# State recurrence in pairs of steps, first loads on two queues and a new engine order, in a kernel that joins windowed attention with a diagonal state-space model

## The chip, the core and the metric

The kernel runs on one core of a Trainium2 chip. The core has five engines that run their own instruction streams and wait for each other by semaphores: TensorE (PE: matmuls, with its weight loads shown apart as PEld), VectorE (DVE), ScalarE (ACT), GpSimd (POOL) and SyncE (SP, which here only issues transfers). Sixteen DMA engines move data. The metric is the time of one execution in microseconds (us), the median over runs.

## The reference

Two independent branches, their outputs joined along the last axis, in bfloat16. S = L = 2048 tokens, D = 448, 16 heads of 28.

```
# A: attention over 8 positions, two apart
q, k, v = split(x @ wqkv)
logits[s, w] = q[s] . k[s - 2w] * 28**-0.5        (w = 0..7, masked where s - 2w < 0)
a = softmax(logits) @ v[s - 2w] @ wo
# B: a complex diagonal recurrence of 448 states
Lam_bar = exp(exp(log_dt) * (Lambda_re + 1j*Lambda_im))
B_bar = ((Lam_bar - 1) / Lam)[:, None] * Bmat
h[t] = Lam_bar * h[t-1] + B_bar @ x[t]
y[t] = 2 * real(Cmat @ h[t]) + x[t] * Dskip
```

## The kernel before

**Branch A.** A's tokens are brought into the layout features x tokens (`xT`, the first 1024 by transposes on TensorE: `XI`, `XA`, `XH`; the rest by transposing DMAs). `QK` and `QS` project to q and k, `qk` and `qh` evict them from PSUM to SBUF, and `P` multiplies, on VectorE, q with k shifted by 2w, for four shifts at once: 28 products of 128x2048. `E_` sums these over each head on TensorE, `lt`, `TR`, `tr` transpose the logits, `sma`, `smb`, `smc` are the softmax, `AL`, `al`, `ad`, `sp` turn the weights into a banded matrix by way of DRAM, `AV` multiplies it with v (`V_`), and `W_` applies wo; `w` evicts and `ow` stores.

**Branch B.** The 448 complex states are 7 groups `g` of 64; real and imaginary parts stand in 128 partitions. The 2048 steps are 512 columns of T = 4 steps, `j` = 0..3. `BU` projects x with B for one step (four steps in two passes of two PSUM banks), and `BR` adds the state of the step before, rotated by Lam_bar (a 128x128 matrix `R[g, 0]`), so that each bank holds the state as if the column began at zero. `z` evicts it. The last step of each pair of columns is joined (`UP`, with the rotation by four steps) and scanned along the 256 pairs by VectorE: `sa` turns into a rotating frame, `sb` is the scan with real decay, `sd` turns back; one call serves two groups (0 and 1, 2 and 3, 4 and 5, and 6 alone). Then the carried state is given back: `DN` and `dn` to the odd columns, and for each of the steps j = 0, 1, 2 a matmul `H_` (128x512) with its own rotation and a VectorE addition `h` (128x512 out of PSUM): 21 of each. `C` multiplies the states of one step and 128 columns with C (7 matmuls of 448 columns, summed in one bank), `c` adds x * Dskip (`xd`) on VectorE and `oc` stores. `ca`, `cs` scale C by Lam's coefficients; `pb` to `pg` compute all coefficients from the three vectors Lambda_re, Lambda_im and log_dt (`raw`); `ty`, `tf`, `ts` make the tables of the rotating frame, `rb` the rotations.

**Order.** Nothing is scheduled by a tool: the string `ORDER` lists every step once, with the PSUM banks it takes behind `@`, and a last `.` (ScalarE) or `=` (VectorE) says who evicts. Each engine runs its own steps in this order, without overtaking. SyncE issues nearly all transfers, in order too: x of the first four token blocks in two transfers, wqkv in slices of 128 columns, and so on; the three parameter vectors are issued by ScalarE as its first work. `WU` is 24 matmuls on zeros at the start.

Of the kernel before, what the change touches and what calls it, by code (L numbers as in the profile page):

```python
# [9 lines left out]
BF16 = mybir.dt.bfloat16  # L10
# [16 lines left out]
SHR = 1.0 - 1e-6  # L27
MAGIC = 12582912.0
# [4 lines left out]
BD WU@0 XI0@12 XI1 xa00= xa01. PP@3 pcopy pa pb pd_ xh0. QS00@4 XH1@5 pc ty5 ty4 pe qk000. pf XA10@6 tf4 tf5 xt1 ts04  # L33
xh1= XA11@7 xa11= xt3 QS10@0 QK021@13 qk010. QK061@24 xa10= QK060 QK020 ts05 pg qh011. QS01@5 qk001. P001 QS11@7
qk020= ts15 qh000. QK041@60 ts25 ty0 QK031@15 P000 qk021. QK030 rb2 tf0 qk030. P020 P021 ts14 QK040 V_100@31 qk011.
P011 qk031. qk041. qh001. ts24 QK050@75 QK051 V_011@02 ts00 ty1 qh010. qk050. V_010 E_00@4 E_02 qk040. tf1 P010 E_01@7
P030 v010. qk051. P051 V_101 v011. hc0 ts01 ts11 V_001@60 P041 V_111@52 rb3 V_110 v110= ts10 ts20 v100. v101. v111.
V_000 v001. v000= P050 ty3 P061 QK100@31 QK110@20 QK101 QK111 xt2 qk111. qk101. V_401@56 V_400 qk100. QK130@01 P031
E_03 E_05 v400. xt0 LC P040 E_04 qk110. v401. QK131 qk130. qk131. QK151@35 QK141@26 QK140 ts21 QK161@01 P060 qk140.
E_06 QK160 lt01 QK150 tf3 P110 ts03 ts13 P101 qk141= lt00 qk150. V_511@27 P100 ty6 qh110. QK121@64 qh111. P111 E_11@3  # L40
# [843 lines left out]
```

## Time and profile before

| | |
|---|---|
| median of 3 runs | 135.06 us (134.78 to 135.12) |
| span of the profiled execution, first to last instruction | 132.7 us |
| what lies around the span (135.06 - 132.7) | 2.4 us |
| ScalarE, GpSimd busy in it | 89.7 us, 19.8 us |
| DMA moved | 22.62 MB, mean 170 GB/s |

The profile is of one execution. The span is what the engines' rows add up to; the rest of the measured time lies around it. A group's line gives busy time (overlaps counted once), the mean length of one instruction, then the idle time of its engine just before them and what ended it. Instructions of one engine overlap by some tens of ns, and matmuls by far more: 42 matmuls of 448 columns end 7.94 us after the first began, while each is shown with 352 ns. So a rate is read from the distance of starts in a timeline, not from the length of one row. Some matmul records are missing, which leaves gaps of 0.2 to 0.4 us that are put down to "issue".

### The profile page before, as it was taken

The numbers are of one execution on the slowest core, as the hardware profiler recorded it, in microseconds if no ns is written. First come the engines' busy times: TensorE is split into PE (matmuls) and PEld (weight loads), VectorE is DVE, ScalarE is ACT, GpSimd is POOL, SyncE is SP. The second block draws the span as 40 slices with busy tenths as digits, with TensorE's granted clock in tenths as the row PEclk, the third lists the DMA queues.
The fourth block names the chain that finished last, engine by engine and source line by source line (L and its number), as shares of the span: only waits on it lengthen the run. The fifth ranks groups of instructions, "written<-read, shape, count | busy, mean of one in ns | idle before, by whom it ended". The sixth has DMA issues, their size and how long they took to land.

```text
span 132.7 us, 2860 instructions
## 1 busy us (share of the span) xinstructions
PE 125.4 (94%) x1068; PEld 63.4 (48%) x1078; DVE 116.9 (88%) x211; ACT 89.7 (68%) x180; POOL 19.8 (15%) x37
## 2 busy tenths in 40 slices
PE   6987999999999999999999999999999999999990
PEld 6642344344333533435335645955954455555550
DVE  5589999999899999999999798999999996969851
ACT  3396499994578999999899899999999110100000
POOL 6801000000000000035599700000000000000000
PEclk9999999999999999999999999999999999999998
DMA  4897998999989998997849599895513301321543
GB/s 109 201 228 159 304 241 147 152 200 212 263 187 214 208 224 215 380 180 134 223 148 185 199 172 373 187 182 70 175 35 110 104 0 38 105 69 39 182 153 110
DMA packets 45348, 22.62 MB, mean 170 GB/s; under 512 B 33239, under 2 KB 44311, under 8 KB 45335
## 3 DMA queue, kind: packets, MB, share of 16 engines
q1 hardware_dynamic: 45272, 22.45, 73.3%
q8 instruction: 8, 0.13, 0.4%
q14 instruction: 5, 0.04, 0.1%
q10 hardware_dynamic: 63, 0.01, 0.0%
HBM read 11.68 MB, written 6.29 MB: 135 GB/s over the span
## 4 chain that ended last, share of the span: by engine, by line
PE 64%; ACT 15%; DVE 9%; SPq 5%; issue 3%; DMA 2%; POOL 0%
PE ps L242 31%; PE ps L771 14%; PE ps L686 4%; PE ps L380 3%; PE ps L752 3%; SPq L131 2%; ACT ctmp L648 2%; ACT oT L113 2%; SPq L137 2%; ACT kf L113 2%; PE ps L511 2%; DMA wq<-in_A_wqkv_dram 2%; PE ps L498 2%; ACT qf L113 2%; DVE hs L727 1%
## 5 line engine op out<-in xcount | busy, mean ns | idle before, releaser
L368 DVE TENSOR_TENSOR pr<-qf,kf 128x2048 bf16<-128x2048 bf16 x24 | 28.3, 1217 | 0.2 <-ACT kf L113 0.2
L242 PE MATMUL ps<-xbuf,BT 128*128 128x512 bf16 (+1 forms) x108 | 23.1, 379 | 0.7 <-issue 0.6
L242 PE MATMUL ps<-xT,wq 128*128 128x512 bf16 (+1 forms) x92 | 20.9, 380 | 1.4 <-DVE xT L113 0.5
L771 PE MATMUL ps<-Cw,Z 128*128 128x448 bf16 x105 | 21.3, 352 | 0.2
L113 ACT CAST Z<-ps 128x512 bf16<-128x512 f32 (+1 forms) x32 | 15.2, 509 | 1.0 <-PE ps L242 0.6
L113 ACT CAST ya<-ps 128x448 bf16<-128x448 f32 (+1 forms) x14 | 7.3, 547 | 11.5 <-issue 10.9
L771 PEld LDWEIGHTS <-Z 128*128 128x128 bf16 x105 | 10.3, 98 | 10.1 <-issue 0.7
L242 PEld LDWEIGHTS <-BT 128*128 128x128 bf16 (+1 forms) x112 | 8.8, 97 | 12.3 <-issue 3.3
L511 PE MATMUL ps<-wo,oT 128*128 128x448 bf16 x64 | 13.8, 353 | 0.2 <-DVE oT L113 0.2
L242 PEld LDWEIGHTS <-wq 128*128 128x128 bf16 (+1 forms) x96 | 7.6, 97 | 13.1 <-issue 4.0
L757 DVE TENSOR_TENSOR Z<-ps,Z 128x512 bf16<-128x512 f32 x21 | 13.5, 680 | 0.4 <-PE ps L752 0.3
L777 DVE TENSOR_TENSOR xbuf<-ps,xnB 128x448 bf16<-128x448 f32 x15 | 8.9, 619 | 4.6 <-PE ps L771 3.8
L242 PE MATMUL ps<-wq,xT 128*128 128x448 bf16 (+1 forms) x64 | 12.1, 353 | 0.0
L841 POOL MEMSET PT<- 128x4320 f32 x3 | 11.1, 3728 | 1.7 <-ACT Z L113 1.7
L113 ACT CAST kf<-ps 128x512 bf16<-128x512 f32 x12 | 6.9, 593 | 4.0 <-PE ps L242 3.9
L648 ACT ACTIVATE ctmp<-Cw,c2t 64x448 f32<-64x448 bf16 x14 | 9.3, 666 | 0.3
L113 ACT CAST oT<-ps 128x512 bf16<-128x512 f32 x16 | 9.0, 614 | 0.1
L511 PEld LDWEIGHTS <-oT 128*128 128x128 bf16 x64 | 6.1, 98 | 6.1 <-DVE oT L113 0.7
L498 PE MATMUL ps<-PT,v_s 128*32 128x135 bf16 (+1 forms) x256 | 8.3, 298 | 0.0
L242 PEld LDWEIGHTS <-xT 128*128 128x128 bf16 (+1 forms) x64 | 5.0, 97 | 6.4 <-issue 2.6
L498 PEld LDWEIGHTS <-v_s 128*32 128x32 bf16 x256 | 7.0, 112 | 0.4 <-issue 0.4
L113 ACT CAST v_s<-ps 128x448 bf16<-128x448 f32 x14 | 7.0, 549 | 0.0
(153 smaller groups left out, 191.1 us busy)
## 6 DMA issues: line engine op xcount, KB each, us to landing
PT<-pd SPq DMA_DIRECT2D x16, 156.0 KB, 4.0
xnB<-in_B_x_dram SPq DMA_DIRECT2D x2, 896.0 KB
out_dram<-ya SPq DMA_DIRECT2D x16, 112.0 KB, 1.8
out_dram<-xbuf SPq DMA_DIRECT2D x15, 112.0 KB, 1.8
pd<-Ak SPq DMA_DIRECT2D x2, 640.0 KB, 3.7
xbuf<-in_A_x_dram SPq DMA_DIRECT2D x2, 448.0 KB
xnB<-in_B_x_dram SPq DMA_DIRECT2D x4, 224.0 KB, 7.0
xnB<-in_B_x_dram SPq DMA_DIRECT2D x4, 192.0 KB, 4.6
```

Of the source, the lines that this page charges most:

```text
L113: (ACT.copy if e == "A" else V.tensor_copy)(o, i)
L242: PE.matmul(o, l, r, start=(first and i == 0), stop=(not first and i == len(pairs) - 1 and not more[s]))
L368: V.tensor_tensor(t[:], q.unsqueeze(1).to_broadcast((128, 4, 512)), k4, ALU.mult)
L380: PE.matmul(acc[s][32 * i:32 * i + 32], E[:, f, ws, :], t[:, i, :], start=(f == 0 and ws == 0), stop=False)
L498: PE.matmul(p[32 * hh:32 * hh + 32, 128 * bl:128 * bl + n], v_s[:, t, 4 * hg + hh, :], PT[:, t % NS, (4 * hg + hh) // HS, (4 * hg + hh) % ...
L511: PE.matmul(p[:, 0:D], late["oT"][:, b // 4, hg, par, 128 * (b % 4):128 * (b % 4) + 128], late["wo"][:, hg, :], start=(hg == 0), stop=(hg ...
L648: ACT.activation(t[a:a + 64, 0:D], Cw[b:b + 64, g, :], ACTF.Copy, scale=c2t[a:a + 64, g:g + 1])
L686: PE.matmul(pp["z", g, j][:], rot(g, 0), late["Z"][:, g, j - 1, :], start=False, stop=True)
L757: V.tensor_tensor(zz, pp.pop(("h", j, g))[:], zz, ALU.add)
L771: PE.matmul(p[:, 0:D], z, Cw[:, g, :], start=(g == 0), stop=(g == G - 1))
L777: V.tensor_tensor(yo, pp.pop(("c", j, ct))[:, 0:D], xnB[:, ct, j, :], ALU.add)
L841: POOL.memset(late["PT"][:, 4 * i:4 * i + 4].rearrange("p t g n -> p (t g n)").bitcast(F32), 0.0)
```

## The change

**State in pairs.** The rotation by -1 (`BACK`) is multiplied into B for the odd steps (`BB`, `bb`: B^T with B's rotation, per group 4 matmuls of 128 columns and one eviction), so the states of steps 0 and 1, and of 2 and 3, share a bank (`BF`, `BX`, `BY`, evicted by `z` after the first step and after the second), and one rotation by two steps (`BR`) stands between the pairs: 7 instead of 21. For the odd steps C is multiplied by the rotation by +1 (`CB`, `cb`). Giving back the carried state, step 2 takes it from the bank of `DN` (`DO`, `do`), and steps 0 and 1 share one rotated copy: `H_` (7 instead of 21) is evicted (`hs`) and added to both steps in one VectorE instruction (`h`, 128x1024, all in SBUF).

**First loads.** SyncE and ScalarE issue half of the first loads each; wqkv comes by 256 columns; the parameter vectors stand on SyncE behind the second half of x. The first tokens' projections are cut in two by 256 tokens (`XT`, `xe`, `QH`), the others are `QF`, `QX`, `QY`. `WU` is the last matmul step.

**Order and memory.** `ORDER` is new throughout, the choice of evicting engine too. The projection's output uses free halves of `xbuf`, and `Ak` of the last band shares `Ak0`.

```diff
-BD WU@0 XI0@12 XI1 xa00= xa01. PP@3 pcopy pa pb pd_ xh0. QS00@4 XH1@5 pc ty5 ty4 pe qk000. pf XA10@6 tf4 tf5 xt1 ts04
+XT00@01 xe00. xe10= XT01 xe01. QH00@2 xe11= QH01 XT10@34 XT11 XH xf1. xf0= QH10@5 xh= LC QF11@6 QF01@7 qk000= PP@0
...
+C31@2 H_3@5 ow10 hs3= ow40 oc32 h3 CH0@7 C22@6 w61. ow61 C13@0 C00@5 c31 c33 c30 C20@2 c13 C02@1 c22 ow70 C21@3 c00
+C12@0 c02 oc30 w31. c21 oc31 C03@4 oc00 oc33 oc13 c20 oc02 ow31 c12 C10@6 oc22 oc20 c10 ch0 oc12 oc21 C01@5 ow41 oc10
+C11@1 CH1@3 c03 c01 oh0 WU@2 oc03 oc01 c11 ch1 oc11 oh1
...
-    for i, vec in enumerate((B_Lambda_re, B_Lambda_im, B_log_dt)):
-        ACT.dma_start(raw[:, i], vec.rearrange("(g p) -> g p", p=64).unsqueeze(1).to_broadcast((G, 2, 64)))
...
     SP.dma_start(xnA[:, 0:2], xA_r[:, 0:2])
-    SP.dma_start(xnA[:, 2:4], xA_r[:, 2:4])
-    w_load(0, 128, 0, D)
-    w_half(0, 0, 128, 0, D)
+    ACT.dma_start(xnA[:, 2:4], xA_r[:, 2:4])
+    w_load(SP, 0, 256)
+    w_load(ACT, D, 256)
+    w_half(SP, 0, 0, 256, 0, D)
+    w_half(ACT, 1, 0, 256, 0, D)
     SP.dma_start(xnA[:, 4:8], xA_r[:, 4:8])
...
+    for i, vec in enumerate((B_Lambda_re, B_Lambda_im, B_log_dt)):
+        SP.dma_start(raw[:, i], vec.rearrange("(g p) -> g p", p=64).unsqueeze(1).to_broadcast((G, 2, 64)))
...
+    def qfull(m, s, c, new):
+        p = pp["qk", 0, m][s]
         for kt in range(3):
+            PE.matmul(p[:, c], wqk(m, slice(0, 128), kt), xT[:, 0, 4 * s + kt, c], start=(new and kt == 0), stop=True,
+                      skip_group_check=True)
...
+    def QH(m, h):
+
+        if h == 0:
+            pp["qk", 0, m] = {0: ps()}
+        qfull(m, 0, slice(256 * h, 256 * h + 256), h == 0)
+        if h:
+            qhalf(m, 0)
...
+    def BB(g):
+
+        p = pp["bb", g] = ps()
+        for f in range(4):
+            PE.matmul(p[:, 128 * f:128 * f + 128], Bn[:, g, 128 * f:128 * f + 128], rot(g, BACK), start=(f == 0), stop=True,
+                      skip_group_check=True)
...
+    def CB(g):
+        p = pp["cb", g] = ps()
+        PE.matmul(p[:, 0:D], rot(g, FWD), Cw[0][:, g, :], start=True, stop=True)
...
+    def BF(g, q, s):
+
+        p, new = zbank(g, q)
+        for f in range(3):
+            PE.matmul(p[:], BT[s][:, g, f, :], xTB[:, q, 4 * s + f, :], start=(new and f == 0), stop=True, skip_group_check=True)
...
-    def BR(g, j):
-        PE.matmul(pp["z", g, j][:], rot(g, 0), late["Z"][:, g, j - 1, :], start=False, stop=True)
+    def BR(g):
+        p, new = zbank(g, 1)
+        PE.matmul(p[:], rot(g, R2), late["Z"][:, g, 1, :], start=new, stop=True, skip_group_check=True)
...
+    def DO(g):
+        PE.matmul(pp["dn", g][:, N2:], rot(g, R4), late["Z3"][:, g, EV:EV + N2], start=False, stop=True, skip_group_check=True)
+
+    @op
+    def do(g):
+        zz = late["Z"][:, g, 2, :]
+        V.tensor_tensor(zz, pp.pop(("dn", g))[:], zz, ALU.add)
+
+    @op
+    def H_(g):
+
+        p = pp["h", g] = ps()
         s = late["Z3"][:, g, OD - 1:OD - 1 + N2]
         s = bass.AP(s.tensor, s.offset, [list(s.ap[0]), [EV - OD + 1, 2], [1, N2]])
-        PE.matmul(p[:], rot(g, j), s, start=True, stop=True)
-
-    @op
-    def h(j, g):
-        zz = late["Z"][:, g, j, :]
-        V.tensor_tensor(zz, pp.pop(("h", j, g))[:], zz, ALU.add)
+        PE.matmul(p[:], rot(g, R2), s, start=True, stop=True)
+
+    @op
+    def hs(g, e):
+        t = pp["hs", g] = late["sc"].tile([128, NC], BF16, tag="hp", name="hp", bufs=2)
+        evict(e, t[:], pp.pop(("h", g))[:])
+
+    @op
+    def h(g):
+        zz = late["Z"][:, g, 0:2, :]
+        V.tensor_tensor(zz, pp.pop(("hs", g))[:].unsqueeze(1).to_broadcast((128, 2, NC)), zz, ALU.add)
...
-            PE.matmul(p[:, 0:D], z, Cw[:, g, :], start=(g == 0), stop=(g == G - 1))
+            PE.matmul(p[:, 0:D], z, Cw[j % 2][:, g, :], start=(g == 0), stop=(g == G - 1))
```

Three places of the new order. The first is SyncE's and the start of VectorE's stream. SyncE before, its first transfers (xbuf is x of branch A, wq the projection's weights):

```order
L139 DMA xbuf<-in_A_x_dram 128x2x448
L140 DMA xbuf<-in_A_x_dram 128x2x448
L131 DMA wq<-in_A_wqkv_dram 128x3x128 x2
L137 DMA wq<-in_A_wqkv_dram 64x2x128
L143 DMA xbuf<-in_A_x_dram 128x4x448
```

SyncE now (ScalarE meanwhile issues the second `128x2x448` of x, the k weights `128x3x256` and one `64x2x256`):

```order
L137 DMA xbuf<-in_A_x_dram 128x2x448
L129 DMA wq<-in_A_wqkv_dram 128x3x256
L135 DMA wq<-in_A_wqkv_dram 64x2x256
L144 DMA xbuf<-in_A_x_dram 128x4x448
L129 DMA wq<-in_A_wqkv_dram 128x3x192 x2
L148 DMA raw<-in_B_Lambda_re_dram 7x2x64
L148 DMA raw<-in_B_Lambda_im_dram 7x2x64
L148 DMA raw<-in_B_log_dt_dram 7x2x64
```

The 128x4x448 of x stands fourth instead of sixth, and the parameter vectors, which were ScalarE's first transfers, stand behind it.

The second place is VectorE up to its first product `pr` of branch A. Before, its last rows ahead of that product are these (the coefficients of C, step `pg`; two steps `tf`, L613 and L614, stand further ahead):

```order
L592 SCALAR_TENSOR_TENSOR c1t<-t_211,cols,den 128x7
L593 TENSOR_TENSOR t_211<-b_209,P_194 128x7
L594 TENSOR_TENSOR t_212<-a_208,P_194 128x7
L595 TENSOR_TENSOR t_211<-t_211,t_212 128x7
L596 SCALAR_TENSOR_TENSOR c2t<-t_211,den 128x7
L368 TENSOR_TENSOR pr<-qf,kf 128x2048
```

Now, right behind the eviction of kf (`pb`, `pe`, `pd_`):

```order
L570 TENSOR_TENSOR are<-dt,P_191 128x7
L571 TENSOR_SCALAR arc<-are 128x7
L572 SCALAR_TENSOR_TENSOR f_192<-dt,P_191 128x7
L590 COPY u_202<-f_192 128x7
L592 TENSOR_SCALAR u_202<-f_192,cols 128x7 x3
L593 TENSOR_SCALAR k_203<-u_202 128x28
L594 SCALAR_TENSOR_TENSOR u_202<-k_203,u_202 128x28
L583 TENSOR_SCALAR fT<-f_192 128x7
L584 TENSOR_SCALAR km<-f_192 128x7
L585 SCALAR_TENSOR_TENSOR fT<-km,fT 128x7
L586 TENSOR_SCALAR fT<-fT 128x7
L389 TENSOR_TENSOR pr<-qf,kf 128x2048 x4
```

The 19 small rows of `pg` and all `tf` now stand behind the first products.

The third place is VectorE from the end of the last scan (`sd6`) on. Before (L757 is `h`, L745 `dn`, L777 `c`):

```order
L734 TENSOR_TENSOR Z_857<-vv,p_1708 128x256
L745 TENSOR_TENSOR Z_857<-ps,Z_857 128x256
L757 TENSOR_TENSOR Z<-ps,Z 128x512
L652 SCALAR_TENSOR_TENSOR Cw<-Cw,c1t,ctmp 128x448
L757 TENSOR_TENSOR Z<-ps,Z 128x512
L777 TENSOR_TENSOR xbuf<-ps,xnB 128x448
L757 TENSOR_TENSOR Z<-ps,Z 128x512 x2
L745 TENSOR_TENSOR Z_857<-ps,Z_857 128x256 x2
L757 TENSOR_TENSOR Z<-ps,Z 128x512 x5
L777 TENSOR_TENSOR xbuf<-ps,xnB 128x448 x3
```

Now, the last rows (L841 is `h`, L845 `xd`, L116 into hp `hs`, L861 `c`, L885 its halves):

```order
L841 TENSOR_TENSOR Z<-hp,Z 128x1024
L845 TENSOR_TENSOR xnB<-xnB,dsk 128x1792
L116 CAST hp<-ps 128x512 x2
L841 TENSOR_TENSOR Z<-hp,Z 128x1024 x2
L845 TENSOR_TENSOR xnB<-xnB,dsk 128x1792
L116 CAST hp<-ps 128x512
L841 TENSOR_TENSOR Z<-hp,Z 128x1024
L861 TENSOR_TENSOR xbuf<-ps,xnB 128x448 x11
L885 TENSOR_TENSOR xbuf<-ps,xnB 128x224
L861 TENSOR_TENSOR xbuf<-ps,xnB 128x448 x3
L885 TENSOR_TENSOR xbuf<-ps,xnB 128x224
```

Before, outputs `c` stand between the `h`, and the last `h` has 7 of the 15 whole `c` and one of the two halves behind it. Now 14 of the 15 and both halves stand behind the last `h`.

More of the change, by code (lines that the diff above doesn't have):

```diff
@@ L835, in pm @@
         if i == 4:
-            for g in (2, 3):
-                POOL.memset(late["Ak"][g].bitcast(F32), 0.0)
+            POOL.memset(late["Ak"][2].bitcast(F32), 0.0)
         elif i == 3:
```

259 lines of the change are left out of this document (140 added, 119 removed).

## Prediction

> **What bounds the kernel now.** First the page's busy shares, then the engines in five stretches (from, to, length; busy time and instructions of each engine; granted clock, DMA share, GB/s).
>
> ```profile
> span 132.7 us, 2860 instructions
> PE 125.4 (94%) x1068; PEld 63.4 (48%) x1078; DVE 116.9 (88%) x211; ACT 89.7 (68%) x180; POOL 19.8 (15%) x37
> ...
> 0.00:14.00 14.00, 11.24 (x80) 6.81 (x82) 10.24 (x43) 8.32 (x21) 5.51 (x30) 1.00 0.74 178
> 14.00:54.00 40.00, 39.47 (x277) 16.03 (x280) 38.59 (x47) 32.96 (x69) 0.11 (x1) 1.00 1.07 216
> 54.00:84.00 30.00, 29.47 (x282) 14.52 (x288) 27.97 (x45) 28.49 (x53) 14.19 (x6) 1.00 0.85 216
> 84.00:104.00 20.00, 19.58 (x301) 12.46 (x294) 19.15 (x43) 18.40 (x37) 0.00 (x0) 1.00 0.57 120
> 104.00:132.70 28.70, 25.61 (x142) 13.56 (x139) 20.96 (x37) 1.50 (x3) 0.00 (x0) 0.99 0.28 90
> ```
>
> TensorE looks like the bound, but from 14 to 104 us VectorE works 85.7 of 90 us too, and both run the same list without overtaking. So I ask where each really waits. VectorE's whole list of waits above 0.15 us in that stretch, in its timeline (start, length, group, and in brackets the wait), with the points used below:
>
> ```profile
> 14.06 1.22 DVE L368 TENSOR_TENSOR pr<-qf,kf 128x2048 bf16<-128x2048 bf16 x1
> ...
> 19.00 3.50 DVE L368 TENSOR_TENSOR pr<-qf,kf 128x2048 bf16<-128x2048 bf16 x3 [0.19 <-ACT kf L113]
> 34.98 1.22 DVE L368 TENSOR_TENSOR pr<-qh_t,kh 128x2048 bf16<-128x2048 bf16 x1 [0.54 <-PE ps L380]
> 73.64 0.69 DVE L113 CAST Z<-ps 128x512 bf16<-128x512 f32 x1 [0.72 <-PE ps L242]
> 80.36 0.43 DVE L745 TENSOR_TENSOR Z<-ps,Z 128x256 bf16<-128x256 f32 x1 [0.45 <-PE ps L739]
> 91.47 0.69 DVE L652 SCALAR_TENSOR_TENSOR Cw<-Cw,c1t,ctmp 128x448 bf16<-128x448 bf16 x1 [0.23 <-ACT ctmp L648]
> ...
> 101.80 0.29 DVE L734 TENSOR_TENSOR Z<-vv,p 128x256 bf16<-128x256 bf16 x1
> ...
> 122.07 0.68 DVE L757 TENSOR_TENSOR Z<-ps,Z 128x512 bf16<-128x512 f32 x1
> ...
> 129.65 0.39 DVE L801 TENSOR_TENSOR xbuf<-ps,xnB 128x224 bf16<-128x224 f32 x1
> ```
>
> Five waits, 2.1 us in 88 us from the first product `pr` (14.06) to the end of the last scan (102.09). VectorE is as full as TensorE there. After that TensorE leads: the last `h` ends at 122.75 and outputs follow to 129.65. The chain that ended last (start, length, engine and line, count) gives TensorE's rates in that stretch and before it:
>
> ```profile
> 44.21 0.45 PE ps L398 x8
> ...
> 80.97 0.11 PE ps L739
> 81.08 0.65 PE ps L752 x3
> ...
> 121.00 7.94 PE ps L771 x42
> ```
>
> So a matmul of 512 columns takes 0.217 us, of 256 0.11, of 448 0.189, of 128 0.056.
>
> **The change on TensorE.** `BR` goes from 21 to 7 and `H_` from 21 to 7: 28 x 0.217 = 6.1 us less. Added: 7 `DO` of 256 columns 0.8, 28 `BB` of 128 1.6, 7 `CB` of 448 1.3, and four half-row matmuls of B that stand alone instead of in pairs (14 passes become 16) 0.4. Net 2.0 us less; the other projections are the same columns in other pieces. `WU` at the end takes 24 x 0.056 = 1.3 us behind the last output matmul, hidden by that output's addition and store (the span ends 3.1 us after 129.65).
>
> **The change on VectorE.** Prices, from the groups (busy, mean ns; then idle before):
>
> ```profile
> L757 DVE TENSOR_TENSOR Z<-ps,Z 128x512 bf16<-128x512 f32 x21 | 13.5, 680 | 0.4 <-PE ps L752 0.3
> L415 DVE TENSOR_TENSOR attn<-attn,m 128x1024 bf16<-128x1024 bf16 x2 | 1.4, 692 | 0.1
> L630 DVE TENSOR_TENSOR R<-Is,co 128x896 bf16<-128x896 bf16 x4 | 4.3, 1083 | 0.0
> L761 DVE TENSOR_TENSOR xnB<-xnB,dsk 128x1792 bf16<-128x1792 bf16 x4 | 4.3, 1082 | 0.0
> L614 DVE SCALAR_TENSOR_TENSOR fr<-kM,fr 128x256 f32<-128x256 f32 x7 | 3.0, 425 | 0.7
> L613 DVE TENSOR_SCALAR kM<-iot,fT 128x256 f32<-128x256 f32 x7 | 2.4, 347 | 0.0
> L113 DVE CAST Z<-ps 128x512 bf16<-128x512 f32 (+1 forms) x3 | 1.8, 601 | 0.7 <-PE ps L242 0.7
> ```
>
> An `h` out of PSUM, an eviction of 512 or a `do` costs about 0.62 (between 13.5 / 21 and 1.8 / 3), a `tf` pair 0.8, an `xd` 1.0. The new `h` (128x1024 in SBUF) has no row: between L415's 0.69, all in bfloat16 with one operand repeated as here, and L630's 1.2 per 1024, which has a float32 factor. I take 0.65, as L415 is the nearer.
>
> In all VectorE hardly gains: 21 `h` (13.0) become 7 `do`, 7 `h` and 3 of the 7 `hs` (10.8), 2.2 less; three more evictions of z by 512 and three by 256 (3.0), one `bb`, one `cb`, one `ci` (1.9) and two `pg` rows are 5.2 more; one q/k eviction, two of v, one of oT and one of ya fewer are 3.0 less. What counts is where the work stands.
>
> *Up to the first product.* The path there, from these rows:
>
> ```profile
> 3.66 0.82 PE L285 MATMUL ps<-ident,xbuf 128*128 128x128 bf16 x6
> 3.69 0.58 SPq L143 DMA_DIRECT2D xbuf<-in_A_x_dram  x1
> 5.91 0.58 ACT L113 COPY xT<-ps 128x512 bf16<-128x512 bf16 x1 [2.29 <-PE ps L287]
> 6.64 0.17 DVE L548 TENSOR_TENSOR are<-dt,P 128x7 f32<-128x7 f32 x1 [0.34 <-ACT dt L544]
> 7.88 0.41 PE L308 MATMUL ps<-ident,xbuf 128*64 128x128 bf16 x4 [0.38 <-DMA xbuf<-in_A_x_dram]
> 8.22 0.84 PE L294 MATMUL ps<-ident,xbuf 128*128 128x128 bf16 x12
> 8.42 0.20 DVE L569 SCALAR_TENSOR_TENSOR u<-k,u 128x35 f32<-128x35 f32 x1
> 11.69 0.18 DVE L580 TENSOR_TENSOR co<-cs,rk 128x28 f32<-128x28 f32 x1
> ```
>
> Transposes begin at 3.65 as now: the first x is issued at the same time. The second eight write banks that wait for the first eviction (0.6), so they start at 5.2, and `QH01` is through at 7.0 to 7.8. The x of tokens 512 to 1023 lands now at 7.88, 4.2 us after its issue at 3.69; it is issued some 1.0 us earlier, with 40% more bytes ahead of it: 7.0 to 7.8. Its 16 transposes end at 8.4 to 9.5, evictions at 9.1 to 10.0, `QF11`, `QF01` (6 x 0.217) at 10.4 to 11.3, the parameters' transposes and `QH11` at 11.1 to 12.1, kf's eviction at 11.8 to 12.7. Then 13 small rows, as many as now from 6.64 to 8.62 (2.0 us). The first product starts at 13.5 to 14.7; I take 14.0, where it starts now. But now VectorE has by then done `pg` (17 rows from 11.69 to 14.06) and two `tf`; after the change it waits instead, since the parameter vectors come late.
>
> *From the first product to the end of the last scan* VectorE gains 19 `pg` rows (2.7), two `tf` (1.6), 2 `do` and an `h` (1.9), 3 + 3 z evictions (3.0), `bb` and `ci` (1.3): 10.5. It loses three q evictions (1.8), two v (1.1), oT (0.6), two ya (1.1), two `xd` (2.0), four old `h` (2.4): 9.0. That is 88.0 + 1.5, less part of the 2.1 us of waits, since a later VectorE finds the others done: I take 1.4 off. End of the scan: 14.0 + 88.1 = 102.1, as now.
>
> *From there to the last `h`*: 2 `w`, a `cs`, a `cb` (2.3), 5 `do` (3.1), 3 `dn` (1.1), 6 `h` (3.9), 3 `xd` (3.0), 3 `hs` (1.8), one `c` (0.6): 15.8 us, and 0.3 for round trips to TensorE. So 118.2, 4.5 us ahead of the present 122.75. But the last `h` now carries steps 0 and 1 of its group, and all eight outputs of these steps wait for it. Behind it stand `C13`, `C00`, `C20`, `C02`, `C21`, `C12`, `C03`, `C10`, `C01`, `C11` and `CH1`: 10 x 7 x 0.189 + 7 x 0.096 = 13.9 us, where now 6.9 us pass from 122.75 to 129.65. 118.2 + 0.1 + 13.9 = 132.2, plus the unchanged 3.1 is a span of 135.3, plus 2.4 around it 137.7 us. That lies on the profiled execution's own span; runs scatter by 0.3 us around the median.
>
> By TensorE's own sum it would reach `C13` at 112.6 (129.65 - 2.0 - 1.1 - 13.9, the 1.1 from the start, below). It waits 5.6 us for VectorE, spread over its evictions and `DN`.
>
> *ScalarE* gets 6 `bb`, 6 `cb`, 4 `hs` and loses few: 7 us more, covered by the 27 us that it idles behind 104. *Band, stores*: their issues move with their producers; the band's round trip (4 + 4 us) has as much room as now.
>
> **Rivals.**
> 1. *TensorE stays the bound.* For it: its rows are solid and its sum falls. At the start it had 7.0 us of matmuls done when its solid run began at 14.5, and would have 5.6 done at 12.0: 1.1 us won. 129.65 - 3.1 = 126.5, span 129.6, 132.0 us. Against it: VectorE would have to save 5.6 us on my sum, and each us that it saves counts fully. Half of that gives 134.9.
> 2. *Cold clock.* Without `WU`, the first projections run slow. The same transposes take 0.82 us for 6 at 3.66 and 0.84 for 12 at 8.22, so TensorE doubles its rate between them; this first product would come 1.0 us later: 138.7. [...]
> 3. *ScalarE holds the end.* `hs` for groups 2, 4 and 6 stand behind projections' evictions; if it falls 2 us behind VectorE, 139.7. Against it: 27 idle us.
> 4. *The gains cancel* (134.7 to 135.4): VectorE's sum 2.5 us too high, as with cheaper small rows and no waits.
>
> **How the numbers follow.** The sum's ends: first product 13.5 or 14.7, waits 2.1 or none off, `ci` 0.2 less, round trips 0 or 1.0: 136.2 to 140.4, and 1 us of pricing error below: 135.4 to 140.4 for the likeliest case. An `h` at L630's price would add 3.9, which I hold unlikely. Chances: the sum 0.52, cold clock 0.08, ScalarE 0.07, cancel 0.10, TensorE's bound 0.23 (in whole, 132.0, or for the greater part, up to 134.5). Below 0.3% (0.4 us) no change can be told. The case of gains that cancel lies mostly inside that, 0.08, and 0.01 on each side. So faster 0.24, same 0.08, slower 0.68. The range reaches into rival 1, half of which lies above 132.6: 132.6 to 140.3.
>
> **What would show it.** Right: VectorE idle between 7 and 12 us and its first `pr` at 13.5 to 14.7; then few waits of VectorE, and TensorE's waits on VectorE's z evictions, `dn` and at `C13` several us in all; last scan near 102, last `h` near 118. Wrong: a first `pr` before 12.5; a new `h` of 0.4 us or 1.2; TensorE without gaps from 12 us on; the last `h` before 114.

## The result and the profile after

The changed kernel takes 146.78 us (median of 4 runs, 145.93 to 147.05) against 135.09 (134.78 to 135.24) of the kernel before, measured beside it: a ratio of 1.0845, 95% interval 1.0798 to 1.0891. It is 11.7 us slower. The forecast, 137.7 us and slower, had the sign and a fifth of the size; the time lies 6.5 us above the upper end of the range.

The page's span, busy shares and granted clock (in 40 slices of 3.6 us) of the changed kernel:

```profile
span 145.0 us, 2915 instructions
PE 127.0 (88%) x1088; PEld 64.2 (44%) x1098; DVE 118.8 (82%) x213; ACT 98.1 (68%) x197; POOL 18.7 (13%) x36
...
PEclk9999998699999999999995999999999999999999
```

TensorE's busy time is 1.6 us more than before, and its idle time (span minus busy) 18.0 instead of 7.3, so it is idle for 10.7 of the 12.3 us of added span: 1.7 of them lie ahead of 14 us, where `WU` no longer runs, and 9.1 between 14 and 104 us. VectorE's busy time rose by 1.9, ScalarE's by 8.4. The engines in the same stretches as before (from, to, length; busy time and instructions of each engine; granted clock, DMA share, GB/s):

```profile
0.00:14.00 14.00, 9.56 (x66) 5.67 (x68) 7.60 (x22) 5.38 (x14) 5.53 (x30) 1.00 0.81 207
14.00:54.00 40.00, 36.30 (x259) 15.26 (x260) 34.24 (x60) 35.11 (x74) 0.00 (x0) 0.96 1.09 210
54.00:84.00 30.00, 26.17 (x193) 10.82 (x190) 27.67 (x36) 25.70 (x46) 13.14 (x6) 0.94 0.43 119
84.00:104.00 20.00, 16.95 (x230) 9.86 (x230) 18.43 (x41) 17.67 (x39) 0.00 (x0) 1.00 0.98 215
```

Between 14 and 104 us TensorE, VectorE and ScalarE each stand still for 9.7 to 11.5 of 90 us; before, TensorE stood for 1.5, VectorE for 4.3 and ScalarE for 10.2. So no engine is full there now; they wait for each other. VectorE's timeline, with its waits in brackets, shows where (the first product, every wait above 0.4 us until the last scan, the one long row, the last row of the last scan's turning back, the last `h` and the last output):

```profile
14.38 4.62 DVE L389 TENSOR_TENSOR pr<-qf,kf 128x2048 bf16<-128x2048 bf16 x4
...
30.87 5.77 DVE L389 TENSOR_TENSOR pr<-qf,kf 128x2048 bf16<-128x2048 bf16 x5 [4.51 <-ACT qh_t L116]
...
53.27 5.77 DVE L389 TENSOR_TENSOR pr<-qf,kf 128x2048 bf16<-128x2048 bf16 x5 [0.48 <-PE ps L401]
...
60.61 1.23 DVE L389 TENSOR_TENSOR pr<-qh_t,kh 128x2048 bf16<-128x2048 bf16 x1 [0.43 <-PE ps L401]
...
63.72 0.69 DVE L446 TENSOR_TENSOR z<-attn 128x512 f32<-128x512 bf16 x1 [0.69 <-ACT attn L440]
...
67.36 3.79 DVE L640 TENSOR_SCALAR kM<-iot,fT 128x256 f32<-128x256 f32 x1
...
81.65 0.76 DVE L116 CAST Z<-ps 128x256 bf16<-128x256 f32 x2 [0.76 <-PE ps L739]
...
96.74 0.43 DVE L814 TENSOR_TENSOR Z<-ps,Z 128x256 bf16<-128x256 f32 x1 [0.95 <-PE ps L808]
...
109.27 0.29 DVE L789 TENSOR_TENSOR Z<-Z,tab 128x256 bf16<-128x256 bf16 x1 [1.75 <-ACT tab L652]
...
112.75 0.29 DVE L803 TENSOR_TENSOR Z<-Z,p 128x256 bf16<-128x256 bf16 x1
...
127.61 0.69 DVE L841 TENSOR_TENSOR Z<-hp,Z 128x1024 bf16<-128x1024 bf16 x1
...
142.04 0.39 DVE L885 TENSOR_TENSOR xbuf<-ps,xnB 128x224 bf16<-128x224 f32 x1
```

Seven waits make 9.6 us, and one row takes 3.8 us where its six fellows take 0.35. The largest wait begins on SyncE. In the timelines of SyncE and TensorE:

```profile
16.25 6.36 SPq L178 DMA_TRANSPOSE xT<-xbuf  x4
...
24.40 1.14 PE L248 MATMUL ps<-xT,wq 64*128 64x512 bf16 x3 [3.08 <-DMA xT<-xbuf]
25.76 4.66 PE L248 MATMUL ps<-xT,wq 128*128 128x512 bf16 x16 [0.22 <-issue]
...
75.42 1.25 PE L734 MATMUL ps<-xbuf,Bn 128*128 128x512 bf16 x3 [2.31 <-ACT Z L116]
...
91.60 3.83 PE L519 MATMUL ps<-PT,v_s 128*32 128x135 bf16 x120 [1.54 <-DMA PT<-pd]
...
104.84 0.41 PE L519 MATMUL ps<-PT,v_s 128*32 128x135 bf16 x8 [2.21 <-DMA PT<-pd]
```

The tokens of A's second half are transposed by DMA and land at 24.3 us. The new order puts `QK161`, the first step that reads them, right behind the first half's work, and TensorE reaches it at 21.3. Everything queued behind it waits too, on TensorE and, through its evictions, on ScalarE and VectorE. The last two rows are waits for the band's round trip through DRAM, which TensorE did not have before.

### The profile page after: what moved, and what is told of

The parts are those of the page before. It is cut to its first block, busy times and chain, and to the rows that moved or that the text cites. A ratio compares the mean times of both kernels' runs of the same rounds, so it can differ in the third digit from the quotient of the medians.

```text
span 145.0 us, 2915 instructions
## 1 busy us (share of the span) xinstructions
PE 127.0 (88%) x1088; PEld 64.2 (44%) x1098; DVE 118.8 (82%) x213; ACT 98.1 (68%) x197; POOL 18.7 (13%) x36
## 4 chain that ended last, share of the span: by engine, by line
PE 40%; ACT 22%; DMA 17%; SPq 9%; DVE 6%; issue 3%; ACTq 0%
PE ps L855 14%; PE ps L248 7%; PE ps L532 6%; PE ps L734 5%; DMA PT<-pd 4%; DMA pd<-oT 4%; DMA xbuf<-in_A_x_dram 4%; ACT ctmp L675 4%; SPq L178 3%; DMA wq<-in_A_wqkv_dram 3%; DVE kM L640 3%; ACT kf L116 2%; SPq L488 2%; DMA xT<-xbuf 2%; ACT v_s L116 2%
## 5 line engine op out<-in xcount | busy, mean ns | idle before, releaser
L248 PE MATMUL ps<-xT,wq 128*128 128x512 bf16 (+1 forms) x61 | 15.1, 410 | 3.5 <-DMA xT<-xbuf 3.1
L855 PEld LDWEIGHTS <-Z 128*128 128x128 bf16 x105 | 10.3, 98 | 9.4
L734 PE MATMUL ps<-xbuf,Bn 128*128 128x512 bf16 x40 | 11.5, 391 | 2.5 <-ACT Z L116 2.3
L248 PE MATMUL ps<-wq,xT 128*128 128x448 bf16 (+1 forms) x64 | 13.5, 352 | 0.2
L116 ACT CAST Z<-ps 128x512 bf16<-128x512 f32 (+1 forms) x26 | 12.6, 515 | 1.3 <-issue 1.2
L861 DVE TENSOR_TENSOR xbuf<-ps,xnB 128x448 bf16<-128x448 f32 x15 | 8.7, 619 | 5.5 <-PE ps L855 5.5
L116 ACT CAST oT<-ps 128x512 bf16<-128x512 f32 x17 | 9.5, 594 | 3.4 <-PE ps L519 3.2
L734 PE MATMUL ps<-xbuf,BT 128*128 128x512 bf16 x38 | 11.5, 399 | 0.2
L855 PE MATMUL ps<-BT,Z 128*128 128x448 bf16 x56 | 11.6, 352 | 0.0
L248 PEld LDWEIGHTS <-wq 128*128 128x128 bf16 (+1 forms) x64 | 5.6, 102 | 12.9 <-issue 8.3
L116 ACT CAST xbuf<-ps 128x448 bf16<-128x448 f32 x14 | 7.2, 548 | 4.8 <-PE ps L532 4.8
L855 PE MATMUL ps<-Cw,Z 128*128 128x448 bf16 x49 | 9.9, 352 | 0.0
L331 PE MATMUL ps<-xT,wq 128*128 128x512 bf16 (+1 forms) x41 | 9.3, 367 | 0.1
L116 ACT CAST v_s<-ps 128x448 bf16<-128x448 f32 x16 | 7.9, 548 | 0.0
```

Source lines behind the costliest of these rows:

```text
L116: (ACT.copy if e == "A" else V.tensor_copy)(o, i)
L248: PE.matmul(o, l, r, start=(first and i == 0), stop=(not first and i == len(pairs) - 1 and not more[s]))
L331: PE.matmul(p[:, c], wqk(m, slice(0, 128), kt), xT[:, 0, 4 * s + kt, c], start=(new and kt == 0), stop=True, skip_group_check=True)
L734: PE.matmul(p[:], BT[s][:, g, f, :], xTB[:, q, 4 * s + f, :], start=(new and f == 0), stop=True, skip_group_check=True)
L855: PE.matmul(p[:, 0:D], z, Cw[j % 2][:, g, :], start=(g == 0), stop=(g == G - 1))
L861: V.tensor_tensor(yo, pp.pop(("c", j, ct))[:, 0:D], xnB[:, ct, j, :], ALU.add)
```

## The experiments

Names are those of the runs; times are medians of four, beside runs of the kernel before on the same chip. Steps are written as in `ORDER`.

**e1 to e4: single waits.** e1 moves one eviction:

```diff
-QK160 qk021. P050 QK100@74 qh110. qk030. ts11 QK110@53 tf4 qk031. E_00@6
+QK160 qk021. P050 QK100@74 qk030. ts11 tf4 qk031. qh110. QK110@53 E_00@6
```

> Changed kernel; ScalarE's eviction qh110, which waits for the tokens of the second half, stands behind qk030 and qk031 instead of ahead of them, and QK110 behind it. Theory (a wait of one engine at the head of its queue): VectorE's wait of 4.5 us at 26.4 us shrinks to at most 0.5, since kf of step qk031 is there by 25; everything on VectorE's path to the last scan comes some 4 us sooner and the time falls to 142.5 to 144. Rival (ScalarE, solid from 27.7 us on, is the bound by then): VectorE's wait goes but ScalarE still stands 3 us for the second half, VectorE waits later instead, and the time stays above 145.5.

146.24 us (145.99 to 146.78), which overlaps the changed kernel's runs, so no gain can be told. The wait stayed, at 4.38 us, but its releaser is now TensorE's `E_` (L401): there are 7 product buffers, and the eighth product needs one that `E_00` gives back, which stands behind the matmuls that wait for the second half. The eviction alone was not what held VectorE.

e2 moves the transposing DMAs ahead of B's x:

```diff
-    x_load(0)
...
         SP.dma_start(xT[:, 1, :, 128 * t:128 * t + 128], xA1[:, t], transpose=True)
+    x_load(0)
```

> Changed kernel; SyncE issues the four transposing transfers of A's second half ahead of the first six loads of branch B's x instead of behind them. Theory: the transposes are issued 1 to 3 us sooner (14 to 15.5 us instead of 16.25), land by 21.5 to 23, TensorE's wait of 3.1 us shrinks to 1 or less, ScalarE's 4.1 and VectorE's 4.5 by as much (2 to 3 us), the time falls to 143.5 to 145. Rival (the load of x itself, not the queue, sets when they start): transposes still at 16, time 146.3 to 147.

151.11 us, a miss on both sides. They were issued at 16.27 as ever, since the load of x itself ends then (the rival), but B's x came 11 us later and B's first passes started at 55.4 instead of 51.1: 4.3 us, the whole loss.

e3 moves one table step of VectorE:

```diff
-BF201 TR1@2 ca3 tf2 BF500@1
+BF201 TR1@2 ca3 BF500@1
...
-smc1 BR2 pm2 z03. ts02
+smc1 BR2 pm2 z03. tf2 ts02
```

> Changed kernel; step tf2 stands behind smc1 on VectorE, after GpSimd's memsets, instead of behind smb0. Theory (the 3.8 us of one kM row is a wait for GpSimd's memset of PT that began 0.1 us before it): all kM rows take 0.35, VectorE wins 3.4 us there, and the time falls to 143 to 144.5. Rival (the row is long for another reason, as its operand fr or the table): the kM row of tf2 is long at its new place too. Second rival (ScalarE and the band's round trip carry the path there): kM short, time above 146.

145.61 us. All `kM` rows take 0.35, so the cause of the long row is right, but of its 3.4 us only 1.2 reach the end. VectorE's timeline in e3:

```profile
68.82 0.43 DVE L432 TENSOR_TENSOR m<-attn 128x512 bf16<-128x512 bf16 x1 [1.61 <-ACT attn L116]
...
75.39 0.35 DVE L640 TENSOR_SCALAR kM<-iot,fT 128x256 f32<-128x256 f32 x1
```

VectorE waits for ScalarE instead, two steps on, but most of the gain is lost by the move itself: ScalarE's table step `ts02` now waits for the late tf2, and evictions of z and of the band stand behind it. In ScalarE's timeline:

```profile
76.23 0.51 ACT L648 ACTIVATE tab<-fr,cols 128x256 bf16<-128x256 f32 x1 [1.98 <-DVE fr L641]
```

At the first eviction of the band (`Ak`), ahead of this wait, e3 is 2.7 us sooner than the changed kernel (71.62 against 74.31), at the second, behind it, 0.7 (80.16 against 80.88). So 1.2 us is what this repair is worth; the long row itself costs more, some 2.7 us (an estimate from the first eviction).

e4 is the three edits together.

> The three edits of the runs before together (qh110 behind qk031, transposes ahead of B's x, tf2 behind the memsets). Theory: the gains add up, 4.5 + 3.4 us and part of the waits on ScalarE, to 137 to 139.5, which is what the prediction's sum gave without these waits. Rival (ScalarE binds from 28 us on): 140.5 to 143.

149.54 us: e2's loss governs.

**e6: the long row, in the kernel before.**

```diff
-smb1 BU100 tf2 z10. BU010@51 z22. pm2 xd0
+smb1 BU100 z10. BU010@51 z22. pm2 xd0 tf2
```

> Kernel before; step tf2 stands one step later on VectorE, behind xd0, so that its kM row starts about 0.8 us behind the start of GpSimd's memset of PT instead of 0.2 us ahead of it. Theory (such a row waits until the running memset ends): kM takes 2 to 3 us instead of 0.35 and everything behind it comes later, time 136.5 to 138. Rival (the long row of the changed kernel had another cause): kM 0.35, time 134.8 to 135.4.

137.03 us, ratio 1.0135 (1.0057 to 1.0214). The timelines of GpSimd and VectorE, first of the changed kernel, then of e6:

```profile
62.88 3.70 POOL L923 MEMSET PT<- 128x4320 f32 x1 [6.23 <-PE ps L405]
66.52 0.85 POOL L921 MEMSET wo<- 128x896 f32 x1
67.31 7.49 POOL L923 MEMSET PT<- 128x4320 f32 x2
```

```profile
64.63 11.12 POOL L841 MEMSET PT<- 128x4320 f32 x3 [1.67 <-ACT Z L113]
...
65.46 3.02 DVE L613 TENSOR_SCALAR kM<-iot,fT 128x256 f32<-128x256 f32 x1
```

In both, the row ends where the running memset of 3.7 us ends within 0.15 us (67.36 + 3.79 = 71.15, and 67.31 + 7.49 / 2 = 71.06; 65.46 + 3.02 = 68.48, and 64.63 + 11.12 / 3 = 68.34). VectorE's other rows under the memsets, among them products of two SBUF tensors, keep their lengths: `attn` times `z` (128x1024) takes 1.22 us under one (at 71.41 in e6) and 1.23 with none running (at 76.94 in the changed kernel). In the kernel before, the row starts 0.2 us ahead of the memset (64.38 and 64.59), takes 0.34 and escapes. Why this row waits and the others do not, no run here shows.

**e5, e7, e8: TensorE's start, and its steps ahead of the second half.** e5 puts `WU` first; e7 puts work that is ready ahead of `QK161`; e8 is e3, e5 and e7.

```diff
-XT00@01 xe00. xe10= XT01
+WU@7 XT00@01 xe00. xe10= XT01
...
-P040 QK161@02 ts01 qk020. qh010. P041 QK160 qk021. P050 QK100@74 qh110. qk030. ts11 QK110@53 tf4
-qk031. E_00@6 xt3 qh101. pg P021 P031 qh100. ts21 E_04 qh111. E_01@1 hc0 QK121@02
+P040 ts01 qk020. qh010. P041 qk021. qk030. qk031. E_00@6 E_01@1 P050 E_04 QK161@02 QK160 QK100@74 qh110. ts11 QK110@53 tf4
+xt3 qh101. pg P021 P031 qh100. ts21 qh111. hc0 QK121@02
```

> Changed kernel; WU (24 matmuls on zeros) is TensorE's first work again instead of its last. Theory (TensorE starts at half rate after idleness, and the first projections ran in that state): the six first projection matmuls of 256 columns take 0.11 us each instead of 0.21, the first product starts at 13.0 to 13.9 instead of 14.4; but VectorE then waits longer at its eighth product, which is set by the transposed second half, so the time stays within 1 us of 146.8. Rival (the first product's start carries through to the end): 1 us or more faster.

146.18 us (145.16 to 146.35), again no clear gain. The first projections run in two groups of three of 0.49 us instead of six in 1.39, and the first product starts at 14.05. VectorE then waits 4.92 us at its eighth product, which starts at 30.95 as before.

> Changed kernel; E_00, E_01, E_04 (with qk030, qk031 ahead of them) stand ahead of QK161 on TensorE instead of behind QK110. Run e1_qh showed that the 4.4 us wait of VectorE is for a product buffer (there are 7), which E_00 gives back, and E_00 stood behind the matmuls that wait for the transposed second half. Theory: VectorE's wait at its eighth product goes (at most 0.5 us), TensorE's gap at 21 us falls under 1.5 us and the granted clock between 14 and 54 us is 1.00; last scan 3 to 5 us sooner, time 142 to 144. Rival (ScalarE, solid from 28 us on, carries the path): VectorE waits for ScalarE's evictions instead, time above 145.

147.63 us, no gain; in time this is the rival, but VectorE's wait moved on to a product buffer that TensorE's sums give back, and not to ScalarE. VectorE's timeline in e7 has the eighth product without a wait at 26.41, and then

```profile
38.26 1.23 DVE L389 TENSOR_TENSOR pr<-qh_t,kh 128x2048 bf16<-128x2048 bf16 x1 [4.53 <-PE ps L401]
```

> Changed kernel with three edits: the E_ steps ahead of QK161, tf2 behind the memsets, WU first. Theory (in-order waits add up): 139 to 142. Rival (ScalarE carries the path): 143.5 or more.

146.02 us, the rival's time, and not clearly under the changed kernel. In e7 and e8 TensorE's waits at 21 us became waits of 2.76 us for ScalarE's evictions of `kf`; B's first passes start at 51.4, no sooner than in the changed kernel (51.1).

**e9: without the rotations' own work.** `BB`, `bb`, `CB`, `cb` are taken out of `ORDER`.

> Changed kernel without the steps BB, bb, CB, cb (the rotations multiplied into B and C are left out, so the odd steps are computed with unrotated B and with unscaled B in place of C). That takes 12 evictions of 6.9 us off ScalarE, two of 1.3 us off VectorE and 2.9 us of matmuls off TensorE. Theory (the new evictions stand on ScalarE, which is solid from 28 to 88 us, and on the way to the band's round trip): bb alone takes 3.5 us out of that stretch, time 141 to 144. Rival, the prediction's own (VectorE's list sets the end, ScalarE's additions are covered): 145.5 to 146.5, VectorE's 1.3 us at most.

141.44 us, ratio 1.0452: 5.3 us less than the changed kernel, the largest gain of all. Not all of it is the rotations': without them the step tf2, at its old place, comes at 64.85 us, 0.2 us ahead of a memset of `PT` (65.05), and its `kM` row takes 0.40, so e9 has neither the long row nor the late table step of e3. Against e3 (145.61) it is 4.2 us, but only 2.3 of them are there at the band's first eviction (69.33 against 71.62), and the second has 4.3 (75.89 against 80.16): the 2.0 between are e3's wait at `ts02`. So the rotations are worth some 2.3 us here, of which VectorE's own rows are 1.3. In ScalarE's timeline the table step of e9 does not wait:

```profile
71.96 0.51 ACT L648 ACTIVATE tab<-fr,cols 128x256 bf16<-128x256 f32 x1
```

From the first product (15.34) to the end of the last scan (107.32) VectorE still waits 6.8 us in six waits above 0.4 us, for TensorE and ScalarE; the kernel before has three, of 1.7 us in all. The largest is 2.22 us at 92.25, for a matmul that TensorE reaches behind a wait of 2.51 us for the band. The last scan ends 5.2 us later than in the kernel before, and what stands behind it takes 1.2 us longer.

**e10, e11: less work for ScalarE, then for VectorE.** e10 is e8 with

```diff
-        ACT.activation(pp["fr", g][:], iot[:], ACTF.Identity, scale=fT[:, g:g + 1])
+        POOL.tensor_scalar(pp["fr", g][:], iot[:], fT[:, g:g + 1], None, ALU.mult)
...
-V_111@72 ci3. P060
+V_111@72 ci3= P060
...
-P061 ci0. E_03
+P061 ci0= E_03
...
-V_110 ci1. V_410
+V_110 ci1= V_410
```

> Changed kernel with the three edits of e8 and, beyond that, ty (7 rows of 0.53 us on ScalarE) on GpSimd and ci0, ci1, ci3 (2.8 us on ScalarE) on VectorE (0.4 us each). Theory (ScalarE carries the path from 27 to 88 us): 6.5 us less on ScalarE gives 3 to 6 us against the 146.0 of e8, so 140 to 143. Rival (VectorE or the transfers carry it): 145.5 to 147.

145.67 us: ScalarE's busy time fell from 96.7 us (e8) to 91.5, and these 5.2 us gave 0.35, less than the runs scatter. But VectorE, which got the copies `ci`, waited 4.36 us for C's load (the row at 36.58 us), where ScalarE had waited before.

> As e10_ty, but the whole of tf is on GpSimd too (three instructions a step instead of VectorE's two), so VectorE loses 5.3 us of rows besides. Theory (ScalarE and VectorE together carry the path): 1 to 4 us less than e10_ty, 137 to 141. Rival (GpSimd's rows are slow, or slow VectorE's products down while they run): products longer than 1.22 us each between 15 and 60 us, time above e10_ty.

156.47 us: GpSimd takes 0.48 to 2.31 us for a `kM` row (four rows between 14 and 60 us) where VectorE takes 0.35; more of it below.

**e12, e13, e15, e16: the copies moved to where the load is there, and the band.** e12 is e3 and e5 with `ty` on GpSimd and

```diff
-V_111@72 ci3. P060
+V_111@72 P060
...
-ci2= TR0@1
+ci2= ci3= ci0= ci1= TR0@1
...
-V_501 CD2 QK151
+V_501 CD2 CD3 CD1 CD0 QK151
```

> Changed kernel with tf2 behind the memsets, WU first, ty on GpSimd, and ci0, ci1, ci3 on VectorE beside ci2 with CD0, CD1, CD3 beside CD2 (in e8 and e10 the copies ci waited for C's load, which lands at 36.7 us, and held their engine). Theory (a series of in-order waits: second half of x at 24, C at 37, then TensorE): the projection's first B passes start by 49.5 instead of 51.2 and the time is 142.5 to 144.5. Rival (nothing before 50 us matters, the loss is made between 54 and 104): 145 to 146.5.

144.86 us (143.49 to 145.66), between theory and rival; B's first passes start at 50.75 in the profiled execution, which took 145.66.

> As e12_cil, with E_00, E_01, E_04 ahead of QK161 (as in e7). Theory: TensorE does them while the second half of x is on its way, B's first passes start by 48.5, time 142 to 144. Rival (e7 and e8 showed no gain from it): within 0.5 us of e12_cil.

144.27 us, the best of the repaired orders that keep the rotations, 2.5 us under the changed kernel but only 0.6 under e12, as the rival had it. TensorE's remaining waits in e13 for the band:

```profile
88.81 3.86 PE L519 MATMUL ps<-PT,v_s 128*32 128x135 bf16 x120 [2.16 <-DMA PT<-pd]
...
101.92 0.41 PE L519 MATMUL ps<-PT,v_s 128*32 128x135 bf16 x8 [2.06 <-DMA PT<-pd]
```

> As e12_cil, with the evictions al3, al2 and the transfers ad3, ad2 ahead of ca0 and ca5 on ScalarE (in the changed kernel they follow 4 us of other rows there, and TensorE waits 2.2 us at 104.8 us for the band that they send). Theory (the band's round trip ends last between 88 and 105 us): TensorE's wait there goes and the time falls 1.5 to 3 us against e12_cil. Rival (VectorE's scans end last there): within 0.5 us of e12_cil.

143.33 to 145.79 us in four runs, so nothing that can be told from e12.

e16 goes further and puts `AL3`, `AL2` on the bank of `AL1` straight behind the softmax:

```diff
-rb3 AL1@5 pm3 pm1 z31. BF401 BR3 ca6 rb1 BF211 z13. BX4031 ts12 al1. BX2150 z32. UP1
+rb3 AL1@5 pm3 pm1 z31. BF401 BR3 al1. AL3@5 ca6 rb1 BF211 z13. al3. BX4031 ts12 ad1 pm0 pm4 AL2@5 BX2150 z32. al2. UP1
...
-AL3@3 BX3141 cb3. z42= BX5061 z62= wo AL2@0 UP2 sp1 pm4 z51= ca0 ca5 z33. cs0 BF510@6 ts13 al3. al2. ad3 BF611
+BX3141 cb3. z42= BX5061 z62= wo UP2 sp1 sp2 z51= ca0 ca5 z33. cs0 BF510@6 ts13 BF611
```

> As e13_cil_E (144.3), with AL3 and AL2, their evictions and the transfers ad1, ad3, ad2, sp2 as soon as the softmax is done, ahead of ca0, ca5 and the last B passes. Theory (from the softmax at 62 us to 106 us the band's round trip through ScalarE and two transfers ends last: PE waits 2.2 and 2.1 us for it): both waits fall under 0.7 us, the last AV ends 3 to 4 us sooner, time 140.5 to 142.5. Rival (TensorE then waits for VectorE's z evictions and scans in the same place): 143.5 to 145.

148.74 us, 4.5 more than e13. The band's last two evictions end some 5 and 3.7 us sooner (82.45 instead of 86.12 us for the last). But `ad1`, which waits for one of them, now stands ahead of `sp0` in SyncE's list, so that `sp0`, which was ready, is issued at 78.93 instead of 73.57, and the first `AV` starts at 90.44 instead of 86.23. A repair of one queue's order cost more in another.

**e14, e17: the first loads alone, in the kernel before.** e14 takes over the new loads of x, wqkv and the parameter vectors, and nothing else.

> Kernel before with the changed kernel's first loads alone (SyncE and ScalarE issue half each, wqkv by 256 columns, the parameter vectors on SyncE behind x); order and state model as before. Theory (the loss lies in the order and in the state model's added evictions, not in the loads): 134.5 to 136.5. Rival (the late parameter vectors and the weights behind them cost the start): first product later than 15.5 us and 137 or more, with that part of the 11.7 us of loss.

140.70 us, ratio 1.0449 (1.0399 to 1.0498): the rival. In e14 the timelines of TensorE and of VectorE (the `kM` row of tf2), and then the windows view of the first stretch:

```profile
9.05 0.57 PE L534 MATMUL ps<-ident,raw 7*128 7x7 bf16 x3 [3.42 <-DMA raw<-in_B_Lambda_re_dram]
...
12.04 1.46 PE L292 MATMUL ps<-ident,xbuf 128*128 128x128 bf16 x12
...
67.94 3.82 DVE L611 TENSOR_SCALAR kM<-iot,fT 128x256 f32<-128x256 f32 x1
```

```profile
0.00:14.00 14.00, 9.27 (x65) 6.25 (x66) 7.24 (x23) 5.93 (x14) 5.53 (x30) 0.78 0.80 209
```

The old order needs the vectors at 5.8 us (`PP`); they come at 9. After that gap TensorE runs at a low clock (0.78 over the stretch, and 1.46 us for 12 transposes), and the shift drops tf2 into a memset. e17 leaves the vectors where they were, on ScalarE ahead of its half of x.

> As e14_before_loads, with the parameter vectors as ScalarE's first transfers, as in the kernel before: only the split of x and wqkv over two queues is new. Run e14 cost 5.7 us: TensorE waited 3.4 us at PP for the vectors, lost its clock (granted 0.78 up to 14 us), first product 3.8 us later, and tf2 fell into a memset (3.4 us). Theory (the vectors' place did that, x and wqkv over two queues do no harm): no wait at PP, clock 1.00, first product at 13.5 to 14.5, time 134.5 to 136. Rival (x and the weights land later): first product past 15, time above 136.5.

138.90 us (138.3 to 140.6). The profiled execution is the slowest of the four (its span is 138.5), so its numbers are that one's: x of the third and fourth block, now behind the three vectors on ScalarE's queue, came at 7.08 us, 2.2 us after TensorE asked, the first product started at 16.28, and tf2 again met a memset (3.83 us). Leaving the vectors on ScalarE is not free in the old order either; that x and the memset are the reason is read from this one execution. In the changed order, where `PP` stands behind `QF01`, e14's loads give a first product at 14.38.

**e18: both gains together.** e13 without the rotations.

> Kernel e13_cil_E (144.3) without BB, bb, CB, cb (as in e9, the rotations multiplied into B and C are left out, so the odd steps are computed without them). Theory (the loss is a sum of separate parts: waits that the order causes, 2.5 us, and the rotations' matmuls and evictions, 4 to 5 us; a rest lies in the order from the softmax to the band): 138.5 to 140.5. Rival (the parts hide each other, and what e9 won and what e13 won is the same time): 141 to 142, as e9 alone.

143.38 us: the rival, and worse than its 141 to 142. What e9 and e13 won is not two parts of a sum. With the repairs e9 lost 1.9 us, and the trace shows where. With tf2 moved to its repaired place, `kM` meets the end of a memset (1.00 us at 73.06), and ScalarE's table step, which does not wait in e9, stands for 2.71 us. In ScalarE's timeline of e18:

```profile
74.64 0.51 ACT L648 ACTIVATE tab<-fr,cols 128x256 bf16<-128x256 f32 x1 [2.71 <-DVE fr L641]
```

It is 2.7 us later than in e9. Behind it the band's second eviction comes at 78.57 instead of 75.89, its store is issued at 79.17 instead of 76.50, and TensorE's 120 matmuls of `AV`, which wait for the band to come back, start at 88.96 instead of 86.81. So the repair of tf2 that paid in e3 costs some 2 us here. Between e13 and e18, which both have the late tf2, the rotations are worth 0.9 us.

TensorE's idle time between 14 and 104 us sums this up: kernel before 1.5, changed 10.6, e3 9.8, e5 12.5, e7 10.4, e8 12.7, e9 9.8, e12 10.0, e13 10.3, e15 9.5, e16 12.6, e18 11.3. No edit of the new order brought it near the old one.

## Why the prediction was wrong, step by step

The forecast was a sum along VectorE, and its terms can be set against the trace one by one:

| step | forecast | measured |
|---|---|---|
| first product | 14.0 (13.5 to 14.7) | 14.38 |
| end of the last scan | 102.1 | 113.04 |
| from there to the end of the last `h` | 16.1 | 15.3 (to 128.30) |
| from there to the last output addition | 14.0 | 13.7 (142.04) |
| from there to the end of the span | 3.1 | 3.0 (145.0) |
| outside the span | 2.4 | 1.8 (146.78) |

Five of the six terms are within 0.9 us. **The step that failed** is the second, "less part of the 2.1 us of waits, since a later VectorE finds the others done: I take 1.4 off". It is 10.9 us short: 0.4 from the start, 8.9 for waits (9.6 instead of 0.7), 3.4 for the row under the memset, and 1.8 the other way, since the rows themselves take less than priced. The rows were priced from durations, and that held: a new `h` takes 0.69 (7 in 4.7 us; 0.65 was assumed). The waits were taken over from the kernel before, though every engine's list was new. The largest could have been suspected ahead of the run by laying the lists beside each other: in the kernel before the transposing DMAs were issued from 19.27 to 24.63, and `QK161`, which needs them, now stood right behind the first half's work; seven product buffers stood ahead of an `E_` behind it. That this would have been enough for the smaller waits is not shown.

The reason that the prediction gave for "slower", eight outputs behind the last `h`, did show: 13.7 us stand between it and the last output addition, where 6.9 did before. But the gain that was to stand against it, a last `h` 4.5 us sooner than 122.75, did not come; it ended at 128.30, 5.6 later. So the sign came mainly from waits that the sum had put at 0.7 us. The range's own ends, added up from their terms, are 136.0 and 140.5 instead of 136.2 and 140.4, and 135.0 instead of 135.4 with the pricing error; that changes nothing in the outcome.

**ScalarE.** "7 us more, covered by the 27 us that it idles behind 104" is wrong in its place: ScalarE's busy time rose by 8.4 us, where 7 were priced, and the twelve evictions stand ahead of 118 us (`bb`'s six between 51 and 61, `cb`'s between 84 and 118), most of them between rows that others wait for, and most of the idle time is behind them. The rotations are worth 0.9 us (e18 against e13) to some 2.3 (e9 against e3, without e3's wait at `ts02`). That ScalarE's load as such is the bound was tried and fell: 5.2 us less of it gave 0.35 (e10), in e12 and e13 with the load's wait out of the way at most some 2.

**The band**, "as much room as now", cost TensorE two waits of 1.5 and 2.2 us.

**TensorE.** Its sum was to fall by 2.0 and rose by 1.6. Part of that is a slower clock: the mean granted clock was 0.976 against 0.997, and matmuls were slow behind some of the waits. The group that takes 4.38 us in e3 (20 matmuls behind a wait of 1.18) took 6.02 behind the wait of 3.08 (24.40 to 30.42), and three matmuls took 1.25 us at 75.42 behind a wait of 2.31, against 0.81 at 69.71 in the same kernel. It is not the whole: in e13, at a mean clock of 0.998, TensorE is busy for 126.6 us all the same, and why its sum did not fall stays open. So the rival "cold clock" did show, as slow matmuls behind a wait, but not at its place: in mid-kernel they added 1.6 us to a wait of 3.08. The 1.0 us that it added for the start was an estimate that no run shows: with `WU` first (e5) the first product came 0.33 us sooner than in the changed kernel, at 14.05, and in e3, with the same first steps as the changed kernel, 1.8 later. Nor did the price reach the end: e3's first product came at 16.18 instead of 14.38, and its first passes of B still started at 50.92 (51.14 in the changed kernel). Which wait has slow matmuls behind it is not shown, and its length alone does not say: 24 matmuls (`E_`) took 2.33 us behind a wait of 2.76 in e7 and 1.54 behind one of 2.76 in e8 (granted clock from 14 to 54 us 0.96 and 1.00); behind 2.38 us in e13 they took 1.54, and behind 2.31 at 75.42 (above) the matmuls were slow.

**The rivals.** TensorE as the bound (132.0) and gains that cancel were far off. ScalarE holding the end was sought behind 104 us; it held the middle.

**What stays open.** Shown are the memset's stall (1.2 us won by e3's repair in the changed kernel, which gives up most of the row's price again; 1.35% in the old one, some 1.8 us) and that the other single waits are worth little by themselves, since the next in line takes their place. The rotations cost 0.9 to some 2.3 us, as the rest of the order stands. The best order, e9, is still 6.1 us above the kernel before, and its trace puts most of this in waits ahead of the end of the last scan; which part of the order makes them is not shown. The repaired orders keep TensorE idle for 9.5 us or more between 14 and 104 us, against 1.5 before, and e18 says that the parts don't add. A table step moved out of the memset's way without making ScalarE wait was not tried, nor were the pairs in the old order, with its spacing of transfers, evictions and scans.

## What to carry to other kernels

In a kernel whose engines run fixed lists, a sum of durations along the fullest engine is right only while its waits are known; after a reordering, lay for each engine the step that needs a transfer or a buffer beside the step that provides it, and price the gap before the rows. Where two engines are nearly full, as here before the change (TensorE 94%, VectorE 88% busy), taking out one wait can move it to the next step; look at the idle time of the bound engine as a whole, not at the longest wait, and at what a moved step makes others wait for (here tf2 and ScalarE's table step). And a place that an old order happened to miss (here a memset of 3.7 us, by 0.2 us) becomes a lottery for every change that shifts it.

## What the runs showed of the hardware that was not expected

VectorE's float32 `TENSOR_SCALAR` from SBUF to SBUF (`kM`), where it started under a GpSimd memset, ran until the memset ended, within 0.15 us: 3.79, 3.02, 3.82 and 3.83 us instead of 0.35 (after, e6, e14, e17). In e16 it started at 74.08, under a memset that ended at 75.17, and took 1.24. GpSimd's rows were longer beside VectorE's products, too. GpSimd's timeline in e11, with VectorE's products running until 23.9 us and rows of 7 elements behind them:

```profile
20.73 2.05 POOL L640 TENSOR_SCALAR kM<-iot,fT 128x256 f32<-128x256 f32 x1
...
25.50 0.48 POOL L640 TENSOR_SCALAR kM<-iot,fT 128x256 f32<-128x256 f32 x1
```

The same instruction took four times as long beside the products. The seven products took 8.63 us together, where five take 5.77 and four 4.62 in the changed kernel: some 0.6 us more than seven at that pace (an estimate).

TensorE's rate at the start differs between executions of the same steps: the second block's 12 transposes took 0.84 us in the changed kernel and 1.46 in e3, and the first product came at 14.38 and 16.18 us, while the granted clock reads 1.00 up to 14 us in both. In TensorE's timelines, the changed kernel's and e3's:

```profile
7.86 0.84 PE L292 MATMUL ps<-ident,xbuf 128*128 128x128 bf16 x12
```

```profile
8.24 1.46 PE L292 MATMUL ps<-ident,xbuf 128*128 128x128 bf16 x12
```
